# A chunked linear-attention and feed-forward kernel: the high parts of g made by casting DMAs, the guard by an accumulating DMA, splits 1,024 columns wide, and a new order of parts

## The chip, the core and the metric

The kernel runs on one core of a Trainium2 chip. The metric is the device time of one execution in microseconds (us). "PE" is TensorE, "DVE" VectorE, "ACT" ScalarE, "POOL" GpSimd, "SP" SyncE, whose queue issues the loads and stores. A measurement of this kernel varies by about 0.1% either way.

## The reference, cut to what matters

```python
def _attn_ref(q, k, v, alpha):              # 4 x 8 heads, 768 steps, head size 48
    for t in range(S):
        state = alpha[:, :, t, :, None] * state + np.einsum('bhd,bhe->bhde', k[:, :, t], v[:, :, t])
        y[:, :, t] = np.einsum('bhd,bhde->bhe', q[:, :, t], state)

def _moe_ref(x, w_in, w_out):               # x: 3072 x 384, w_in: 384 x 2048, w_out: 2048 x 384
    h = x @ w_in
    sp = np.maximum(h, 0.0) + np.log1p(np.exp(-np.abs(h)))
    g = h * erf(sp)
    return (g @ w_out).astype(np.float32)

x = attn_out.transpose(0, 2, 1, 3).reshape(B * S, H * D)
return _moe_ref(x, w_in, w_out)
```

The weights arrive as 64-bit floats, everything else as 32-bit floats.

## The kernel before

**Attention.** The sequence is cut into 24 chunks of 64 steps for two of the four batches (`Chunk`). A chunk's parts: `la`, `lq`, `lv` load alpha, k and q, and v; `a1` is the running product of alpha (one scan on DVE); `a2` and `a3` scale k by its reciprocal and q by it; `a4` makes the scores `pS` and the state update `pu` on PE, masks the scores (`sT`), updates the state `T` and turns k (`pn`); `a5` makes the output `py` and hands it on as two parts, `x_hi` and `x_lo`. In `a2`, ACT takes first a Relu of the running product above a bound (the "guard": its sum is 0 unless a value is too large), then the logarithm and the exponential that give the reciprocal.

**Feed-forward.** Two chunks give one block of 256 tokens, 12 blocks (`Moe`). Each product is made of three products of rounded parts: high times high, high times low, low times high. A block's hidden 2,048 columns go in four groups of 512, stored as tiles of 128 x 1,024. For each group: `H` (two halves; PE, then a copy to `hs`), `U`, `L1`, `G` on ACT (functions of two tables: `U` and `G` use one, `L1` and the logarithm and exponential of `a2` the other, and each change of table is a table load), `L2` and `Z` on DVE, which leave g in `hs`. `O` (two halves) splits g: `gh` is its rounded copy (ACT, or DVE where the list says `v:`), `gl` the rest (DVE), 512 columns each; then PE adds twelve products of 384 columns to the sums `acc`. `out` stores the block.

**Weights.** `wi_n` (12 pieces) and `wo_n` (16) load a piece of a weight, turn 64-bit into 32-bit floats (ACT and DVE) and split it into `wi_hi`, `wi_lo`, `wo_hi`, `wo_lo`.

**Order.** The order is written out by hand in `SCHED`: a list of the parts, taken one step each. Every engine runs its instructions in the order in which the list made them, and an instruction that waits holds up all behind it on its engine. Most tiles of 128 x 1,024 (`kq`, `hs`, `s`, `w`, `t`, weights on their way) come from one pool, `big`; `gh` and `gl` have buffers of their own, two each. After the list comes the test of the guards (`top`, `count`), which decides whether the slow general branch is run; it isn't with these inputs.

Of the kernel before, what the change touches and what calls it, by code (L numbers as in the profile page):

```python
# [33 lines left out]
a2_1 a2_1 a2_1 a4_0 a4_0 a2_1 wi_1 v:wi_1 wi_1 wi_2 wi_2 wi_6 wi_6 v:wi_6 a2_2 a2_2 a2_1 wi_6 lv_0 lv_1 a5_0 a5_0 a2_2  # L34
a5_0 wi_1 a4_0 a4_0 wi_0 wi_0 wi_6 a2_2 a5_0 a2_2 wi_1 wi_1 v:wi_0 wi_0 wi_4 wi_4 v:wi_4 wi_4 a4_1 a4_1 a4_1 a4_1 wi_0
wi_5 wi_5 v:wi_5 wi_5 wi_4 wi_3 wi_3 v:wi_3 wi_0 wi_7 wi_7 v:wi_7 a5_0 a5_1 wi_4 a5_1 a5_1 wi_0 wi_3 a5_1 wi_8 wi_8
v:wi_8 a5_1 la_3 H_0_0_1 H_0_0_1 wi_5 a4_1 wi_5 H_0_0_0 H_0_0_0 wi_3 wi_9 lq_2 wi_9 v:wi_9 wi_3 a1_3 a2_3 wi_4 wi_9
a2_2 a3_2 a4_2 wi_3 wi_11 H_0_0_1 wi_9 wi_5 wi_11 a2_3 v:wi_11 wi_11 wi_10 wi_10 v:wi_10 wi_10 wi_9 H_0_1_0 a4_2 a4_2
a2_3 wo_2 wo_2 a2_3 wi_11 lv_2 a2_3 wi_10 lq_3 a2_3 H_0_0_0 U_0_0 a4_2 a4_2 la_4 wi_6 wi_7 a3_3 v:wo_2 a5_2 a5_2 a5_2
a5_2 wo_0 wi_10 wi_10 wi_11 wi_11 wi_9 wi_8 H_0_1_0 H_0_1_0 H_0_1_1 H_0_1_1 H_0_1_1 wo_0 U_0_1 L1_0_1 a4_3 a4_3 a4_3  # L40
v:wo_0 wi_8 wi_8 H_0_3_1 H_0_3_0 H_0_3_1 H_0_3_1 wi_7 wi_7 a1_4 a2_4 a2_4 H_0_3_0 H_0_3_0 lv_3 lv_4 a5_3 a5_3 wi_6
a4_3 wi_8 wi_7 wo_2 lq_4 a5_3 a2_4 a5_2 L1_0_0 wo_2 wo_2 lq_5 a5_3 a4_3 H_0_2_0 H_0_2_0 H_0_2_0 a2_4 L1_0_0 L1_0_0
H_0_2_1 H_0_2_1 H_0_2_1 wo_10 wo_10 a3_4 a2_4 a5_3 a2_4 a4_4 wo_2 la_5 H_1_1_0 H_1_1_0 a1_5 L1_0_1 L2_0_0 wo_7 wo_7
L1_0_1 wo_0 wo_10 a2_5 wo_3 wo_0 a4_4 a4_4 L2_0_1 L2_0_0 H_1_0_1 H_1_1_0 L2_0_1 a2_5 a2_5 a2_5 v:wo_7 wo_7 H_1_0_1
H_1_0_1 a5_4 a5_4 a5_4 a5_4 lv_5 wo_0 wo_0 H_1_0_0 a3_5 G_0_0 Z_0_0 a2_5 a4_4 wo_1 wo_7 wo_3 H_1_0_0 H_1_0_0 a2_5
v:wo_3 wo_1 v:wo_1 a4_4 H_1_1_1 H_1_1_1 H_1_1_1 G_0_1 wo_5 wo_5 v:wo_5 Z_0_0 O_0_0_0 Z_0_1 H_1_2_0 wo_4 wo_4 wo_6
H_1_2_0 H_1_2_0 v:wo_4 a4_5 a4_5 a4_5 U_0_2 wo_4 wo_6 v:wo_6 U_0_3 H_1_3_0 H_1_3_0 wo_1 wo_4 wo_4 H_1_3_0 la_6 a4_5
H_1_2_1 H_1_2_1 H_1_2_1 lv_6 a5_5 wo_5 wo_6 H_1_3_1 H_1_3_1 a1_6 a2_6 wo_5 a5_4 wo_5 wo_1 wo_1 wo_3 O_0_0_0 wo_3 a5_5
a5_5 wo_1 a5_5 a5_5 O_0_0_0 O_0_0_0 H_2_3_1 wo_10 H_2_3_1 O_0_0_1 O_0_0_1 wo_10 Z_0_1 a2_6 a4_5 wo_3 lq_6 wo_6 a2_6
a2_6 H_1_3_1 wo_5 H_2_2_0 wo_8 wo_10 a2_6 O_0_0_1 wo_3 wo_8 a2_6 a3_6 O_0_0_1 a4_6 L1_0_2 wo_13 v:wo_8 wo_8 H_2_3_1  # L50
L1_0_2 v:wo_13 wo_4 v:wo_13 wo_10 wo_8 L1_0_3 a4_6 L1_0_2 wo_8 wo_8 wo_7 H_2_2_0 wo_7 a4_6 a4_6 wo_9 v:wo_9 L1_0_3
wo_6 wo_6 H_2_2_0 H_2_2_1 H_2_2_1 L1_0_3 L2_0_2 H_2_3_0 H_2_3_0 O_0_1_0 O_0_1_1 O_0_1_0 O_0_1_1 v:wo_9 wo_9 H_2_2_1
U_1_0 L2_0_2 H_2_3_0 G_0_2 la_7 a1_7 L2_0_3 O_0_1_0 O_0_1_0 wo_11 wo_11 v:wo_11 wo_9 wo_9 H_2_1_0 Z_0_2 la_8 wo_9
Z_0_2 H_2_1_0 H_2_1_0 L2_0_3 wo_11 wo_13 wo_11 H_2_0_0 H_2_0_0 v:H_2_0_0 a2_7 G_0_3 U_1_1 wo_13 a2_7 a2_7 a2_7 H_2_0_1
H_2_0_1 a5_6 a5_6 a5_6 O_0_1_1 O_0_1_1 a5_6 lq_7 a3_7 a2_7 wo_11 wo_11 a2_7 a4_6 O_0_2_0 O_0_2_0 O_0_2_1 O_0_2_1 wo_13
lv_7 H_2_0_1 H_2_1_1 H_2_1_1 L1_1_1 wo_15 wo_15 v:wo_15 H_2_1_1 L1_1_0 a4_7 a1_8 a4_7 a4_7 wo_12 wo_12 a5_6 O_0_2_0
O_0_2_0 v:wo_12 L1_1_0 Z_0_3 wo_15 lv_8 a4_7 L1_1_0 a5_7 Z_0_3 a5_7 a5_7 a5_7 a5_7 O_0_2_1 O_0_2_1 H_3_0_0 wo_12 a2_8
# [692 lines left out]
```

## Time and profile before

| | us |
|---|---|
| median of three runs | 527.58 (527.17 to 527.93) |
| the profiled execution: its time | 526.75 |
| its span, first to last instruction | 525.0 |
| what lies around the span | 1.75 |
| PE busy | 499.5 (95%) |
| DVE busy | 497.3 (95%) |
| ACT busy | 485.1 (92%) |

How to read it: the span is what an instruction can change. Three engines are busy for over nine tenths of it. PE's matmuls overlap, so that a busy PE can still be held up a little at the start of each group of matmuls.

### The profile page before, as it was taken

The numbers are of one execution on the slowest core, as the hardware profiler recorded it, in microseconds if no ns is written. First come the engines' busy times: TensorE is split into PE (matmuls) and PEld (weight loads), VectorE is DVE, ScalarE is ACT, GpSimd is POOL, SyncE is SP. The second block draws the span as 40 slices with busy tenths as digits, with TensorE's granted clock in tenths as the row PEclk, the third lists the DMA queues.
The fourth block names the chain that finished last, engine by engine and source line by source line (L and its number), as shares of the span: only waits on it lengthen the run. The fifth ranks groups of instructions, "written<-read, shape, count | busy, mean of one in ns | idle before, by whom it ended". The sixth has DMA issues, their size and how long they took to land.

```text
span 525.0 us, 16780 instructions
## 1 busy us (share of the span) xinstructions
PE 499.5 (95%) x7386; PEld 481.5 (92%) x7386; DVE 497.3 (95%) x715; ACT 485.1 (92%) x700; POOL 2.3 (0%) x14
## 2 busy tenths in 40 slices
PE   1699999999999999999999999999999999999994
PEld 1599999989999999999999999999999999999994
DVE  6999999999999999999999999999899999999993
ACT  6999999999999999989999899998898999999680
POOL 1000000000000000000000000000000000000000
PEclk9999999999999999999999999999999999999998
DMA  8976353341313203413012311123103120000001
GB/s 296 346 284 237 105 161 114 125 151 41 127 37 93 90 30 107 156 55 134 2 58 67 117 37 38 59 72 109 44 23 121 43 79 26 8 1 30 28 4 37
DMA packets 17936, 48.44 MB, mean 92 GB/s; under 512 B 1984, under 2 KB 5056, under 8 KB 17856
## 3 DMA queue, kind: packets, MB, share of 16 engines
q1 hardware_dynamic: 17856, 47.29, 26.6%
q8 instruction: 60, 0.98, 0.8%
q14 instruction: 20, 0.16, 0.1%
HBM read 42.57 MB, written 4.72 MB: 90 GB/s over the span
## 4 chain that ended last, share of the span: by engine, by line
PE 48%; ACT 25%; DVE 18%; issue 4%; DMA 3%; SPq 0%; DVEq 0%; ACTq 0%
PE acc L495 25%; PE ph L429 18%; ACT s L214 6%; ACT w L214 3%; ACT L213 3%; PE py L364 3%; ACT hs L220 3%; DVE t L458 2%; DVE gl L484 2%; ACT r L214 2%; DVE w L460 2%; DMA A<-in_alpha_dram 2%; ACT wbuf L220 2%; ACT wbuf L532 2%; DVE s L469 2%
## 5 line engine op out<-in xcount | busy, mean ns | idle before, releaser
L429 PE MATMUL ph<-x_hi,wi_hi 128*128 128x256 f32 x576 | 165.8, 288 | 1.8 <-ACT x_hi L220 1.1
L429 PE MATMUL ph<-x_lo,wi_hi 128*128 128x256 f32 x576 | 161.6, 281 | 1.1 <-issue 0.9
L429 PE MATMUL ph<-x_hi,wi_lo 128*128 128x256 f32 x576 | 161.3, 280 | 0.2 <-issue 0.2
L495 PE MATMUL acc<-wo_hi,gh 128*128 128x384 f32 x384 | 130.9, 341 | 0.0
L495 PE MATMUL acc<-wo_hi,gl 128*128 128x384 f32 x384 | 129.9, 338 | 0.8 <-DVE gl L484 0.6
L495 PE MATMUL acc<-wo_lo,gh 128*128 128x384 f32 x384 | 129.1, 336 | 0.0
L429 PEld LDWEIGHTS ph<-x_hi,wi_hi 128*128 128x128 f32 x576 | 109.0, 189 | 5.4 <-ACT hs L220 1.9
L429 PEld LDWEIGHTS ph<-x_hi,wi_lo 128*128 128x128 f32 x576 | 109.8, 191 | 1.0 <-issue 1.0
L429 PEld LDWEIGHTS ph<-x_lo,wi_hi 128*128 128x128 f32 x576 | 109.1, 189 | 0.6 <-DVE x_lo L395 0.5
L214 ACT ACTIVATE s<-s 128x1024 f32<-128x1024 f32 x96 | 100.1, 1054 | 6.2 <-DVE t L458 5.9
L495 PEld LDWEIGHTS acc<-wo_hi,gl 128*128 128x128 f32 x384 | 72.2, 188 | 2.6 <-DVE gl L484 2.4
L495 PEld LDWEIGHTS acc<-wo_hi,gh 128*128 128x128 f32 x384 | 72.2, 188 | 1.2
L495 PEld LDWEIGHTS acc<-wo_lo,gh 128*128 128x128 f32 x384 | 72.2, 188 | 0.0
L484 DVE TENSOR_TENSOR gl<-hs,gh 128x512 fp32r<-128x512 f32 x96 | 65.0, 689 | 6.5 <-ACT gh L220 1.7
L213 ACT ACT_TABLE_LOAD x52 | 66.7, 1283 | 0.9
L471 DVE SCALAR_TENSOR_TENSOR hs<-s,hs 128x1024 f32<-128x1024 f32 x48 | 58.6, 1222 | 0.7
L458 DVE TENSOR_TENSOR t<-s,w 128x1024 f32<-128x1024 f32 x48 | 58.2, 1219 | 1.0 <-ACT w L214 0.8
L469 DVE TENSOR_TENSOR s<-s,w 128x1024 f32<-128x1024 f32 x48 | 58.4, 1220 | 0.6
L460 DVE SCALAR_TENSOR_TENSOR w<-t,w 128x1024 f32<-128x1024 f32 x48 | 58.3, 1220 | 0.3
L220 ACT ACTIVATE hs<-ph 128x512 f32<-128x512 f32 x85 | 49.3, 590 | 3.3 <-PE ph L429 2.8
L214 ACT ACTIVATE w<-s 128x1024 f32<-128x1024 f32 x48 | 50.6, 1057 | 0.6
L214 ACT ACTIVATE s<-hs 128x1024 f32<-128x1024 f32 x48 | 50.4, 1058 | 0.4
(66 smaller groups left out, 719.3 us busy)
## 6 DMA issues: line engine op xcount, KB each, us to landing
kq<-in_qk_dram SPq DMA_DIRECT2D x24, 512.0 KB, 3.7
raw_v<-in_v_dram SPq DMA_DIRECT2D x24, 448.0 KB, 4.1
A<-in_alpha_dram SPq DMA_DIRECT2D x24, 260.0 KB, 3.3
wst<-in_moe_w_in_dram SPq DMA_DIRECT2D x12, 512.0 KB, 9.5
wst<-in_moe_w_out_dram SPq DMA_DIRECT2D x16, 384.0 KB, 3.5
out_dram<-o SPq DMA_DIRECT2D x24, 192.0 KB, 1.9
```

Of the source, the lines that this page charges most:

```text
L213: nc.scalar.preload_act_table_set(table)
L214: nc.scalar.activation(*args, **kw)
L220: nc.scalar.activation(out, in_, AF.Copy, scale=scale)
L364: nc.tensor.matmul(out=py[i][c0 : c0 + 32, kt, :], lhsT=left[r0 : r0 + rows, at0 : at0 + 32], rhs=right[r0 : r0 + rows, pair, i, :], start ...
L429: nc.tensor.matmul(out=o, lhsT=wt[:, kt, fs], rhs=xt[:, kt, :], start=n == 0, stop=n == 3 * KT - 1)
L458: nc.vector.tensor_tensor(out=t, in0=s, in1=w, op=ALU.mult)
L460: nc.vector.scalar_tensor_tensor(out=w, in0=t, scalar=2.0, in1=w, op0=ALU.add, op1=ALU.mult)
L469: nc.vector.tensor_tensor(out=s, in0=s, in1=w, op=ALU.mult)
L471: nc.vector.scalar_tensor_tensor(out=h, in0=s, scalar=RT2 / 2, in1=h, op0=ALU.subtract, op1=ALU.mult)
L484: nc.vector.tensor_tensor(out=gl.rearrange("p a t -> p (a t)"), in0=gg, in1=ghf.bitcast(F32), op=ALU.subtract)
L495: nc.tensor.matmul(out=self.acc[tt][:, :DM], lhsT=gt[:, u, ts], rhs=wt[:, f, :], start=f == 0 and n == 0, stop=f == NF - 1 and n == 2,)
L532: nc.scalar.activation(z, low.bitcast(U32), AF.Copy, scale=0.937 * 2.0**-29)
```

## The change

The guard's Relu leaves ACT: instead a DMA that POOL issues (`ac`) adds each chunk's running product to a tile `sums`, and the largest sum is tested at the end. `O` loses its splits. `E` makes `gh` for all 1,024 columns of a group, in blocks 0 to 10 by a DMA that POOL issues and that casts on its way (block 11: a copy on ACT or DVE); `D` makes `gl` for all 1,024 columns on DVE, as before from `hs` and `gh`. `gh` and `gl` now come from `big`, which has 20 buffers, not 19. Block 11 has six groups, of 4, 4, 2, 2, 2 and 2 column blocks of 128, not four of 4. The branch for `TURNED` is in the code and used nowhere, since `TURNED` is empty. The whole list `SCHED` is new.

```diff
+LAST = (4, 4, 2, 2, 2, 2)
+BY_DMA, TURNED = (0, 1, 2, 3, 4, 5, 6, 7, 8, 9, 10,), ()
 SCHED = """
-la_0 a1_0 la_1 la_2 a1_1 a1_2 lq_0 a3_0 a2_0 a2_0 a2_0 a2_0 a2_0 a2_0 wi_2 wi_2 v:wi_2 wi_2 lq_1 a3_1 wi_2 a2_1 wi_1
...
+la_0 a1_0 a2_0 a2_0 la_1 a1_1 lq_0 a3_0 a2_0 a2_0 a2_1 a2_1 a2_0 la_2 a1_2 a2_1 lq_1 a3_1 a2_1 a4_0 a4_0 wi_1 wi_1
...
-    NBIG, NA = 19, 3
+    NBIG, NA = 20, 3
...
+        def ac(self):
+            nc.gpsimd.dma_start(out=sums, in_=self.A.rearrange("p s t -> p (s t)"), accum_op=ALU.add)
+            yield
+
...
-            nc.scalar.activation(r, A, AF.Relu, bias=-AHI, accum_out=flags[:, self.n, 1:2])
-            yield
             act(LNEXP, r, A, AF.Ln)
             yield
...
+            self.sizes = LAST if n == NBLK - 1 else (4,) * (NF // 4)
...
+        def E(self, g):
+            self.gh[g] = self.pl.w.tile([P, self.sizes[g] * TB], F32R, name="gh", tag=self.pl.tag("gh"))
+            if self.n in BY_DMA:
+                nc.gpsimd.dma_start(out=self.gh[g], in_=self.hs[g])
+            else:
+                copy(self.gh[g], self.hs[g])
+            yield
+
+        def D(self, g):
+            self.gl[g] = self.pl.w.tile([P, self.sizes[g] * TB], F32R, name="gl", tag=self.pl.tag("gl"))
+            nc.vector.tensor_tensor(out=self.gl[g], in0=self.hs[g], in1=self.gh[g].bitcast(F32), op=ALU.subtract)
+            yield
+
         def O(self, g, half):
-            sl = slice(half * 512, (half + 1) * 512)
-            gg = self.hs[g][:, sl]
-            gh = self.pl.gp.tile([P, 2, TB], F32R, name="gh", tag="gh")
-            ghf = gh.rearrange("p a t -> p (a t)")
-            copy(ghf, gg)
-            yield
...
+    for k, z in enumerate((flags, sums)):
+        nc.vector.tensor_reduce(out=top[:, k : k + 1], in_=z, op=ALU.max, axis=mybir.AxisListType.X)
```

Three places of the engines' orders. The first is ACT at the start of the program, before the change; `r` is the reciprocal of `a2`, `wst` and `wbuf` a weight on its way:

```order
L266 ACT_TABLE_LOAD
L266 ACTIVATE r,flags<-A 128x512
L213 ACT_TABLE_LOAD
L214 ACTIVATE r<-A 128x512
L214 ACTIVATE r,flags<-r 128x512
L220 ACTIVATE wbuf<-wst 128x512
L532 ACTIVATE wbuf<-wst 128x512
L266 ACTIVATE r,flags<-A 128x512
```

The same place of the change:

```order
L207 ACT_TABLE_LOAD
L208 ACTIVATE r<-A 128x512
L208 ACTIVATE r,flags<-r 128x512
L208 ACTIVATE r<-A 128x512
L208 ACTIVATE r,flags<-r 128x512
L214 ACTIVATE wbuf<-wst 128x512
L574 ACTIVATE wbuf<-wst 128x512
```

The Relu (the first `r,flags<-A`) and the second table load are gone, and the reciprocal of chunk 1 (the third and fourth ACTIVATE) now stands ahead of the first weight.

The second place is DVE before, where the fourth group of block 0 gets its last operands: the `wo_lo` (the last row but one stands for three) are splits of weights that `O` of that group reads, the first and the last row its two `gl`:

```order
L484 TENSOR_TENSOR gl<-hs,gh 128x512
L540 SCALAR_TENSOR_TENSOR wbuf<-wbuf 128x384 x2
L536 SCALAR_TENSOR_TENSOR wbuf<-wbuf 128x384
L554 TENSOR_TENSOR wo_lo<-wbuf,wo_hi 128x384
L540 SCALAR_TENSOR_TENSOR wbuf<-wbuf 128x384
L222 CAST wo_hi<-wbuf 128x384
L554 TENSOR_TENSOR wo_lo<-wbuf,wo_hi 128x384 x3
L484 TENSOR_TENSOR gl<-hs,gh 128x512
```

The same place of the change, up to the last operand of that group:

```order
L508 TENSOR_TENSOR s<-s,w 128x1024
L578 SCALAR_TENSOR_TENSOR wbuf<-wbuf 128x384
L582 SCALAR_TENSOR_TENSOR wbuf<-wbuf 128x384
L275 TENSOR_TENSOR kq<-kq,rw 128x512
L510 SCALAR_TENSOR_TENSOR hs<-s,hs 128x1024
L596 TENSOR_TENSOR wo_lo<-wbuf,wo_hi 128x384
L525 TENSOR_TENSOR gl<-hs,gh 128x1024
L497 TENSOR_TENSOR t<-s,w 128x1024
L596 TENSOR_TENSOR wo_lo<-wbuf,wo_hi 128x384
```

One wide `gl` stands where two narrow ones stood, and instructions of other groups and of a later chunk (`s`, `hs` and `t` of 1,024 columns, `kq`) now stand between the last operands of this group.

The third place is DVE of the change in block 3, group 2, with the tiles' numbers: `hs_2126` is g of that group, `gh_3641` the output of its casting DMA:

```order
L510 SCALAR_TENSOR_TENSOR hs_2126<-s_3213,hs_2126 128x1024
L499 SCALAR_TENSOR_TENSOR w_3507<-t_3614,w_3507 128x1024
L525 TENSOR_TENSOR gl_3663<-hs_2063,gh_3583 128x1024
L216 CAST x_hi_3286<-py_3511 128x3x64
L508 TENSOR_TENSOR s_3503<-s_3503,w_3507 128x1024
L510 SCALAR_TENSOR_TENSOR hs_2412<-s_3503,hs_2412 128x1024
L525 TENSOR_TENSOR gl_3672<-hs_2126,gh_3641 128x1024
```

Before, `gh` was made by ACT or DVE, in two instructions of 512 columns. Now DVE has five instructions between g (first row) and the `gl` that needs the cast copy (last row), and POOL's DMA is to be made between the two.

## Rows read from the trace of the kernel before

**Rows 1.** Windows by stage: stretch, length, busy us of each engine (instructions), PEclk, DMA share, GB/s.

```profile
0.00:31.00 31.00, 15.65 (x322) 13.76 (x323) 26.42 (x43) 26.06 (x53) 2.35 (x14) 1.00 0.90 324
31.00:124.00 93.00, 90.89 (x1715) 87.00 (x1714) 91.09 (x158) 91.99 (x166) 0.00 (x0) 1.00 0.45 150
124.00:200.00 76.00, 75.55 (x1081) 73.23 (x1080) 74.54 (x102) 75.64 (x107) 0.00 (x0) 1.00 0.25 83
200.00:350.00 150.00, 149.31 (x2314) 144.46 (x2313) 145.80 (x199) 143.72 (x196) 0.00 (x0) 1.00 0.22 71
350.00:518.00 168.00, 167.21 (x1969) 162.57 (x1964) 158.93 (x216) 147.16 (x183) 0.00 (x0) 1.00 0.13 42
518.00:525.00 7.00, 0.85 (x5) 0.53 (x4) 0.56 (x1) 0.49 (x1) 0.00 (x0) 0.74 0.19 64
```

**Rows 2.** Groups by form, PE: total busy us, mean ns of one, idle before.

```profile
L429 PE MATMUL ph<-x_hi,wi_hi 128*128 128x256 f32 x576 | 165.8, 288 | 1.8 <-ACT x_hi L220 1.1 <-ACT hs L220 0.5
L429 PE MATMUL ph<-x_hi,wi_lo 128*128 128x256 f32 x576 | 161.3, 280 | 0.2 <-issue 0.2
...
L495 PE MATMUL acc<-wo_hi,gh 128*128 128x384 f32 x384 | 130.9, 341 | 0.0
L495 PE MATMUL acc<-wo_lo,gh 128*128 128x384 f32 x384 | 129.1, 336 | 0.0
```

**Rows 3.** Timeline of PE, ACT, DVE, the start: start us, busy us, work [idle before].

```profile
10.62 1.98 PE L298 MATMUL pS<-kq 48*64 48x64 f32 x32 [10.62 <-DVE kq L278]
...
26.09 0.58 PE L429 MATMUL ph<-x_hi,wi_hi 128*128 128x256 f32 x1 [1.13 <-ACT x_hi L220]
...
4.97 0.63 ACT L266 ACTIVATE r<-A 128x512 f32<-128x512 f32 x1 [2.88 <-DVE A L260]
5.51 0.19 ACT L266 ACTIVATION_READ_ACCUMULATOR r<-A 128x1 f32 x1
5.71 1.28 ACT L213 ACT_TABLE_LOAD   x1
...
3.70 3.51 DVE L260 TENSOR_TENSOR_SCAN A<-A,lower 128x520 f32<-128x520 f32 x3 [3.70 <-DMA A<-in_alpha_dram]
...
16.73 1.29 DVE L540 SCALAR_TENSOR_TENSOR wbuf<-wbuf 128x512 int32<-128x512 int32 x2
...
25.86 0.62 DVE L395 TENSOR_TENSOR x_lo<-py,x_hi 128x192 fp32r<-128x192 f32 x2
```

**Rows 4.** Timeline of DVE and PE where the fourth group of block 0 begins.

```profile
121.43 1.49 DVE L554 TENSOR_TENSOR wo_lo<-wbuf,wo_hi 128x384 fp32r<-128x384 f32 x3
...
123.41 0.34 PE L495 MATMUL acc<-wo_hi,gh 128*128 128x384 f32 x1
```

**Rows 5.** Groups by form, DVE and ACT.

```profile
L484 DVE TENSOR_TENSOR gl<-hs,gh 128x512 fp32r<-128x512 f32 x96 | 65.0, 689 | 6.5 <-ACT gh L220 1.7 <-DMA out_dram<-o 0.9 <-DVE gh L222 0.5
...
L222 DVE CAST gh<-hs 128x512 fp32r<-128x512 f32 x49 | 20.6, 422 | 0.9 <-PE acc L495 0.2
...
L213 ACT ACT_TABLE_LOAD x52 | 66.7, 1283 | 0.9
...
L220 ACT ACTIVATE gh<-hs 128x512 fp32r<-128x512 f32 x47 | 28.7, 625 | 9.5 <-PE acc L495 7.3 <-DVE hs L471 2.1
...
L214 ACT ACTIVATE s<-hs 128x1024 f32<-128x1024 f32 x48 | 50.4, 1058 | 0.4
```

**Rows 6.** Chain that ended last, two of its links: start us, us, work.

```profile
473.64 6.36 PE ph L429 x54
...
290.62 2.27 DVE t L458 x2
```

**Rows 7.** DMA issues: queue, count, KB each, median us from issue to landing.

```profile
kq<-in_qk_dram SPq DMA_DIRECT2D x24, 512.0 KB, 3.7
...
A<-in_alpha_dram SPq DMA_DIRECT2D x24, 260.0 KB, 3.3
wst<-in_moe_w_in_dram SPq DMA_DIRECT2D x12, 512.0 KB, 9.5
```

More of the change, by code (lines that the diff above doesn't have):

```diff
@@ L227, in gla_moe @@
     nc.gpsimd.memset(T, 0.0)
+    nc.gpsimd.memset(sums, 0.0)
     Tv = T.rearrange("p (i a d) -> p i a d", i=NI, a=NP)[:, :, :, :D]
@@ L348, in a5 @@
                 moe.alloc_x()
+            if self.n in TURNED:
+                py = [ps_at.tile([P, 512], F32, name="pz", tag="at") for _ in range(2)]
+                sums = [(vx, HD, self.sT)]
+                if not self.first:
+                    sums.append((T, D, self.Q))
+                for pair in range(NP):
+                    for n, (left, rows, right) in enumerate(sums):
+                        for par in range(2):
+                            for i in range(NI):
+                                r0 = (par ^ i) * HD
+                                at0 = (i * NP + pair) * HD
+                                nc.tensor.matmul(
+                                    out=py[par][i * HD : (i + 1) * HD, pair * D : (pair + 1) * D],
+                                    lhsT=right[r0 : r0 + rows, pair, i, :], rhs=left[r0 : r0 + rows, at0 : at0 + D],
+                                    start=n == 0, stop=n == len(sums) - 1, tile_position=(r0, i * HD),
+                                )
+                yield
+                t = at.tile([P, KT, 2, 2, HD // 2], F32, name="yt", tag="sT")
+                for par in range(2):
+                    copy(
+                        t[:, :, par].rearrange("p k h d -> p h k d"),
+                        py[par][:, : NP * D].rearrange("p (h k d) -> p h k d", h=2, k=KT),
+                    )
+                    yield
+                px = ps_at.tile([P, 512], F32, name="px", tag="at")
+                for kt, k in enumerate((0, 2, 1)):
+                    nc.tensor.transpose(
+                        px[:, kt * P : (kt + 1) * P], t[:, k].rearrange("p b h d -> p (b h d)"), ident
+                    )
+                yield
+                yield from moe.put_all(px, self.n % 2)
+                return
             py = [ps_at.tile([P, KT, TC], F32, name="py", tag="at") for _ in range(NI)]
@@ L377, in __init__ @@
             self.x = None
-            self.hs, self.w, self.s = [None] * NG, [None] * NG, [None] * NG
+            self.sizes = LAST if n == NBLK - 1 else (4,) * (NF // 4)
+            self.at = [sum(self.sizes[:g]) for g in range(len(self.sizes))]
+            self.hs, self.w, self.s, self.gh, self.gl = ([None] * len(self.sizes) for _ in range(5))
         def alloc_x(self):
@@ L398, in put, with put_all @@
                 yield
+        def put_all(self, px, s):
+            at = [z.rearrange("p k (i j t) -> p k i j t", i=NI, j=2)[:, :, :, s] for z in self.x]
+            y = px[:, : KT * P].rearrange("p (k i t) -> p k i t", k=KT, i=NI)
+            copy(at[0], y)
+            yield
+            nc.vector.tensor_tensor(out=at[1], in0=y, in1=at[0].bitcast(F32), op=ALU.subtract)
+            yield
         def turn(self, y, c, pool, tag):
@@ L630, in general @@
                     m.turn(y[:, 0, :], c, ph, "h")
-                for g in range(NG):
-                    for part in (m.H(g, 0), m.H(g, 1), m.U(g), m.L1(g), m.L2(g), m.G(g), m.Z(g), m.O(g, 0), m.O(g, 1)):
+                for g in range(len(m.sizes)):
+                    for part in (m.H(g, 0), m.H(g, 1), m.U(g), m.L1(g), m.L2(g), m.G(g), m.Z(g), m.E(g), m.D(g), m.O(g, 0), m.O(g, 1)):
                         for _ in part:
```

248 lines of the change are left out of this document (117 added, 131 removed).

## The prediction

> **What bounds the kernel now.** I read first the windows by stage [rows 1]: cut where the first feed-forward matmul begins (before 31 us), where the fourth group of block 0 is added (124), where the attention thins out (350) and where the output is left (518). TensorE (PE) is idle for 15.35 us of the first stage and 6.15 of the last, and for only 2.11, 0.45, 0.69 and 0.79 us of the four between, 4.04 in all. Its clock is 1.00, the 2.4 GHz level, up to 518 us. So PE's own work, 7,386 matmuls, sets the end; the change keeps every one of them. Next come the groups by form [rows 2]: of the four products listed, the first of each triple takes longer than the others that do the same (288 against 280 ns in 576 matmuls, 341 against 336 in 384). That is a small delay at the start of a group, (8 x 576 + 5 x 384) ns = 6.5 us in all, which a busy PE hides. PE could give at most 4.0 + 6.5 us between 31 and 518 us, the start and the end apart.
>
> Then who is beside it: VectorE (DVE) is busy 91.09 of 93 and 74.54 of 76 us up to 200 us, then 145.8 of 150 and 158.9 of 168; ScalarE (ACT) likewise, then 147.2 of 168 [rows 1]. The timelines show where that counts. At the start PE waits for the chain scan, Relu, table load, reciprocal, k, to 10.62 us, and its first `ph` at 26.09 waits for the two parts of x [rows 3]. At 123 us the last `wo_lo` splits end at 122.92 and PE takes their group at 123.41 [rows 4]: there DVE is just in time, and every microsecond more on it counts. After 200 us DVE runs ahead; what is left there are short hand-overs from ACT and DVE to PE.
>
> **The change, part by part.** *Engine sums.* On DVE go 49 casts (20.6 us) and 96 narrow `gl` (65.0) [rows 5]; 46 wide `gl` at 1.22 and 4 narrow ones at 0.69 come (58.9, the wide one taken as `t` of the same shape; two of those in a row end 2.27 us after the first began, 1.14 each [rows 6]). By the order 6 copies of `ph` (0.69 each at most), 3 casts of g and 3 outputs move onto it, about 7 us. DVE: -20.6 - 65.0 + 58.9 + 7 = -20 us. On ACT go 24 Relus of 0.63 and their reads of 0.19 [rows 3], 19.7 us, and 47 narrow `gh`, 28.7 [rows 5]; in come 22 table loads (74 stand in the order, 52 before) at 1.283, 28.2 us, and a few wide copies of block 11 at about 1.06 (as the ACT operation of the same shape [rows 5]), at most 7. ACT: at least -13 us. Both were below PE's sum and fall further: this alone moves nothing but the waits.
>
> *Start.* On ACT the Relu, its read and the second table load leave the first chain: 0.63 + 0.19 + 1.28 = 2.1 us [rows 3], so PE's first `pS` comes near 8.6. This gains little by itself, because the first `ph` then waits for DVE: up to its last `x_lo` DVE has, by the order, 4 scans of 1.17, 24 operations of 512 columns at 0.60 and 6 short ones of 0.27, which after the 3.70 us of loading is 24.4; before it was 3 scans and 27, 25.1 by the same sum and 26.1 in fact. An earlier weight is the other bound: one more 512-KB load stands ahead of it, 1.6 us at the 324 GB/s of that stage [rows 1]. Taken at nothing; -1 to +2.
>
> *Fourth group of block 0.* Here the order decides, since DVE is just in time [rows 4]. Ahead of this group's last operand DVE had 9 scans, 84 operations of 512 columns, 17 of 1,024, 48 of 384 and 27 short ones; now 10, 80, 25, 48 and 25. That is 1.17 - 4 x 0.60 + 8 x 1.14 - 2 x 0.27 = +7.4 us. But PE is given more to do ahead of it: 4 more half-steps of `H` of 9 matmuls at 0.118 (54 in 6.36 us [rows 6]) and one `a4` more at 2.0 [rows 3], +6.2 us. Net +1.2 us; -1 to +3, with the start.
>
> *Dense stretch.* From about 180 us on DVE and ACT have together 30 us less to do against the same PE work, and wide splits mean 50 hand-overs of `gl`, not 96. What can go is 10.5 us (above). The first matmul of a group has always to wait for something, so I take away at most the idle time and about half of the 6.5, and of this range of 0 to 8 us the middle: -4.0.
>
> *Casting DMAs.* No row shows one. Nearest from below: 512 KB of `kq`, 3.7 us from issue to landing; from above: 512 KB of weights, 9.5, taken while the start's loads crowd the queues [rows 7]. DMA share after 31 us is 0.45 falling to 0.13 [rows 1], so I take it near the lower row, 3.7 to 5. What hides it: the DVE work between g and its `gl`. In the order of block 3, group 2 that is `w`, another `gl`, a short cast, `s`, `hs`: 4 x 1.14 + 0.27 = 4.8 us, and this is the shortest of the 44. Worked out likewise, 4 are under 6 us, 12 under 7, 15 under 8 and 22 under 9.5. So at 3.7 to 4.8 us the hand-over costs nothing; beyond, DVE waits, and behind `gl` on it wait the next groups' `s`, `t` and `hs`, then ACT, then PE. Only blocks 0 to 3 have no lead to cover it; there the waits add up to 8 us of DVE at 7 us a DMA, 16 at 8, 33 at 9.5.
>
> *Guard.* Each `ac` moves 260 KB as the load of `A` does, 3.3 us [rows 7], and waits for the one before. All but the last are far from the end. The test of `sums` stands on DVE before the last groups' splits; the last `ac` is issued near them, so a cost of 0 to 2 us is possible; taken 0, since three or four in a row at 3.3 us still land before the last two groups.
>
> *End.* The last matmul, output and store are the same work: 6.15 us [rows 1].
>
> *Sum.* The profiled execution took 526.75 us, 0.83 below the median shown. 526.75 + 1.2 - 4.0 = 523.95 for a profile; with the 0.83, 524.8 us.
>
> **The rivals.** *Slow cast (slower).* The casting DMA takes 7 us or more, because it reads and writes SBUF and POOL must issue it behind the `ac`. At 7 us DVE waits 8.3 us more in blocks 0 to 3, 524.8 + 8.3 = 533; at 8 us 541. It decides from about 6.2 us, where the waits reach the 4.0 gained. For it: 9.5 stands in the rows, and no casting DMA does; against: the row of the same bytes at a quiet time is 3.7.
>
> *Nothing given back (no change).* PE's small waits are those of each group's own first operand and stay; the 10.5 us don't shrink, and +1.2 at the fourth group is made up elsewhere. 527 to 528.6. For it: PE is 99% busy between 31 and 518 us already; against: the idle time is put down to ACT's and DVE's hand-overs.
>
> *Late weights.* More loads in the first 31 us (DMA share 0.90 [rows 1]) delay the first `ph` by 2 to 3 us and nothing makes it up: 528.5 to 531.
>
> *DVE keeps POOL from issuing.* A row speaks of two kinds of DVE work: the cast of 512 columns takes 0.422 us, the subtraction of as many 0.689 [rows 5]. If any DVE instruction kept POOL's DMA from being made, each of the 44 would begin only when DVE stops at its `gl`: 44 x 3.7 = 163 us, less the 48 us that DVE has free after the change (525 - 477): about 640 us. If only the fast casts do, nothing is seen: 46 of the 49 casts of g go away.
> The Trainium skill, SBUF — State Buffer, section "SBUF: two separate sides", says that a DMA issued by GpSimd can't get its descriptors written while VectorE runs an operation in a two-port fast mode, and names the copy of 32-bit floats within SBUF as one. Read broadly, with every operation between g and `gl` in such a mode, it is this rival; read narrowly, with the casts alone, the forecast stands, and 0.422 against 0.689 us speaks for the narrow reading. No trace here shows such a DMA of POOL.
>
> **How the numbers follow.** Forecast 0.55 (521 to 526.4), no change 0.20, slow cast 0.17, late weights 0.06, POOL kept out 0.02. The time is the forecast's, 524.8. The range, 521.0 to 531.0, reaches from 8 us given back (526.75 + 0.83 + 1.2 - 8 = 520.8) over no change and late weights to a cast of some 6.8 us; outside are about 0.05 below and 0.12 above. A measurement here can't tell 0.2%, 1.05 us, from no change. Faster: 0.55; same: 0.22 (no change and a little of late weights); slower: 0.23.
>
> **What would show it.** *Start:* first `pS` near 8.6 us, first `ph` 25 to 27. *Fourth group of block 0:* its first matmul near 130, with DVE busy up to it. *Dense stretch:* PE idle below 2 us between 200 and 518 us, and 288 and 341 ns nearer to 280 and 336. *Casting DMA:* from issue to landing under 5 us, and no idle time of DVE ended by it; 6 us or more, or DVE idle at `gl` in blocks 0 to 3, shows it wrong. *End:* last matmul to the end of the span 6 us as before, with no wait of DVE for `sums`. Wrong would be above all a cast slower than 6.2 us, a tile of the common pool that comes free late, so that the cast is issued late, or a new wait at the last block's six groups.

## The result, and the profile after

The change takes 530.12 us (median of 12 runs, 529.65 to 534.91) against 527.43 before (12 runs): slower, by a ratio of 1.006 (1.0047 to 1.0073). The profiled execution has a span of 528.7 us against 525.0, 3.7 more. Single runs spread wider than the 0.1% named at the start (before: 526.62 to 528.98).

The windows by stage of the change, cut as in [rows 1]; the columns are the same:

```profile
0.00:31.00 31.00, 18.65 (x433) 16.35 (x436) 25.45 (x43) 19.00 (x37) 5.48 (x18) 1.00 0.96 325
31.00:124.00 93.00, 88.77 (x1611) 85.30 (x1599) 90.85 (x150) 92.00 (x157) 6.48 (x9) 0.98 0.63 194
124.00:200.00 76.00, 75.52 (x1233) 72.59 (x1232) 73.42 (x91) 75.49 (x99) 7.87 (x12) 1.00 0.50 154
200.00:350.00 150.00, 150.00 (x2226) 146.11 (x2227) 143.76 (x175) 141.97 (x176) 15.63 (x24) 1.00 0.50 148
350.00:518.00 168.00, 164.40 (x1905) 161.61 (x1899) 149.65 (x179) 147.51 (x170) 12.08 (x20) 1.00 0.28 92
518.00:528.70 10.70, 3.83 (x23) 3.50 (x21) 0.56 (x1) 0.49 (x1) 0.00 (x0) 0.83 0.13 44
```

PE's idle time falls by 3.0 us in the first stage, where it does 433 matmuls instead of 322, and by 0.7 between 200 and 350 us. It grows by 2.1 us between 31 and 124 us and by 2.8 between 350 and 518. PE's busy time is 1.7 us more, though the matmuls are the same: in the second stage the clock is 0.98 on the mean.

Busy and idle time leave out the small delays that a busy PE hides. So I worked out from the records of the matmuls how far PE is behind its own work: the start of a matmul, less what those ahead of it take back to back (0.117 us for each `ph`, 0.173 for each `acc`, and so on: the medians between starts, the same in all the kernels). In us, at the same amount of work done:

| work of PE done | 15 | 23 | 100 | 240 | 350 | 420 | 480 (end) |
|---|---|---|---|---|---|---|---|
| before | 23.5 | 23.6 | 28.2 | 32.5 | 35.2 | 37.4 | 38.7 |
| the change | 21.9 | 27.4 | 29.9 | 34.4 | 37.8 | 40.0 | 41.7 |
| the change, test at the end (below) | 21.9 | 27.6 | 29.8 | 34.4 | 37.2 | 38.1 | 38.3 |

Other prices for the short matmuls move the entries by up to 3.5 us, but what is read from the rows below by at most half a us.

This shows where the time goes. Up to 15 us of work (36.9 us after the start) the change is 1.6 us ahead. Then it loses 5.5 us within 8 us of work. From 23 us of work to the end the kernel before falls another 15.1 us behind, the change with its test at the end 10.7. So 4.4 us are gained behind the start: 2.4 of them up to 100 us of work (some 130 us after the start), 2.0 after it. The change as it is loses most of this again after 240 us of work.

The place of the first loss, in the timelines of ACT, DVE and PE of the change:

```profile
35.55 1.28 ACT L207 ACT_TABLE_LOAD   x1
36.84 1.06 ACT L208 ACTIVATE s<-hs 128x1024 f32<-128x1024 f32 x1
37.81 0.61 ACT L214 ACTIVATE wi_hi<-wbuf 128x512 fp32r<-128x512 f32 x1
...
38.45 1.29 DVE L596 TENSOR_TENSOR wi_lo<-wbuf,wi_hi 128x512 fp32r<-128x512 f32 x2 [1.19 <-ACT wi_hi L214]
...
39.80 0.38 PE L468 MATMUL ph<-x_hi,wi_lo 128*128 128x256 f32 x1 [2.42 <-DVE wi_lo L596]
45.47 0.33 PE L393 MATMUL py<-sT,raw_v 64*32 64x64 f32 x11 [0.82 <-issue]
```

On ACT a table load and the first group's `U` stand ahead of a `wi_hi`, DVE's `wi_lo` waits for it, and PE for that. At 45.47 PE waits again, for nothing that the profile shows. The windows of the change there:

```profile
35.00:40.00 5.00, 2.58 (x71) 2.33 (x72) 3.81 (x7) 4.94 (x6) 0.00 (x0) 1.00 1.03 298
40.00:45.00 5.00, 4.65 (x133) 4.27 (x132) 4.96 (x11) 5.00 (x11) 0.84 (x1) 0.66 1.04 347
```

After the 2.42 us without work the granted clock is 0.66: by the trace's records 3.4 us at the 1.2 GHz level from 40.4 us on. A `ph` starts every 0.21 us there and every 0.117 after it, so the stretch costs about half its length, 1.7. So 2.7 (from one matmul's start to the next) + 1.7 + 1.0 make up 5.4 of the 5.5.

The second loss, in the waits of DVE and of PE late in the change (us in total, times, longest):

```profile
DVE top L711 <- ACT r L208: 2.9, 1, 2.9
DVE top L711 <- DMA sums<-A: 2.8, 1, 2.8
...
PE pS L295 <- DVE kq L275: 1.5, 1, 1.5
...
PE acc L537 <- DVE o L218: 1.0, 1, 1.0
```

`top` is the test of the guards. It is the one piece of the program that isn't in the hand-written list, so the scheduler chose its place: on DVE ahead of the last chunk's work, where it stops at 436.8 us for ACT's reciprocal and at 490.5 for the last accumulating DMA. Behind it stand `kq`, for which PE waits at 442 us, and DVE's work before the output copy `o`, for which PE waits at 504. Before, the same `top` stood at 426.6 us, with no wait.

The transfers, from the DMA issues and the group of `gl` of the change:

```profile
gh<-hs POOLq DMA_DIRECT2D x44, 512.0 KB, 2.9
...
sums<-A POOLq DMA_DIRECT2D x24, 260.0 KB, 4.7
wst<-in_moe_w_in_dram SPq DMA_DIRECT2D x12, 512.0 KB, 10.5
```

```profile
L525 DVE TENSOR_TENSOR gl<-hs,gh 128x1024 fp32r<-128x1024 f32 (+1 forms) x50 | 58.6, 1175 | 0.4
```

The casting DMA lands in 2.9 us, and DVE loses 0.4 us ahead of all 50 `gl`. The accumulating DMA takes 4.7.

### The profile page after: what moved, and what is told of

The parts are those of the page before. It is cut to its first block, busy times and chain, and to the rows that moved or that the text cites. A ratio compares the mean times of both kernels' runs of the same rounds, so it can differ in the third digit from the quotient of the medians.

```text
span 528.7 us, 16811 instructions
## 1 busy us (share of the span) xinstructions
PE 501.2 (95%) x7386; PEld 485.5 (92%) x7386; DVE 483.7 (91%) x635; ACT 476.5 (90%) x636; POOL 47.5 (9%) x83
## 3 DMA queue, kind: packets, MB, share of 16 engines
q1 hardware_dynamic: 17856, 47.29, 27.4%
## 4 chain that ended last, share of the span: by engine, by line
PE 46%; ACT 28%; DVE 15%; issue 6%; DMA 4%; SPq 0%; POOL 0%; DVEq 0%; ACTq 0%; POOLq 0%
PE acc L537 21%; PE ph L468 17%; ACT s L208 7%; ACT L207 5%; PE py L393 3%; ACT w L208 3%; ACT hs L214 3%; DMA sums<-A 2%; DVE t L497 2%; PE pS L295 2%; DVE w L499 2%; DVE hs L510 2%; DMA raw_v<-in_v_dram 2%; DVE gl L525 2%; ACT r L208 2%
## 5 line engine op out<-in xcount | busy, mean ns | idle before, releaser
L208 ACT ACTIVATE s<-s 128x1024 f32<-128x1024 f32 (+1 forms) x100 | 101.2, 1021 | 7.3 <-DVE t L497 6.8
L508 DVE TENSOR_TENSOR s<-s,w 128x1024 f32<-128x1024 f32 (+1 forms) x50 | 58.8, 1175 | 8.7 <-ACT s L208 7.4
L497 DVE TENSOR_TENSOR t<-s,w 128x1024 f32<-128x1024 f32 (+1 forms) x50 | 58.6, 1176 | 2.7 <-ACT w L208 2.5
L510 DVE SCALAR_TENSOR_TENSOR hs<-s,hs 128x1024 f32<-128x1024 f32 (+1 forms) x50 | 58.7, 1178 | 0.8
L499 DVE SCALAR_TENSOR_TENSOR w<-t,w 128x1024 f32<-128x1024 f32 (+1 forms) x50 | 58.7, 1177 | 0.7
L525 DVE TENSOR_TENSOR gl<-hs,gh 128x1024 fp32r<-128x1024 f32 (+1 forms) x50 | 58.6, 1175 | 0.4
L518 POOL DMA_DIRECT2D gh<-hs x44 | 23.6, 537 | 368.2 <-DVE hs L510 78.1
L214 ACT ACTIVATE hs<-ph 128x512 f32<-128x512 f32 x79 | 46.0, 588 | 9.1 <-PE ph L468 9.1
L208 ACT ACTIVATE s<-hs 128x1024 f32<-128x1024 f32 (+1 forms) x50 | 50.9, 1022 | 2.5 <-DVE hs L216 1.1
```

The source lines that it names most:

```text
L208: nc.scalar.activation(*args, **kw)
L214: nc.scalar.activation(out, in_, AF.Copy, scale=scale)
L497: nc.vector.tensor_tensor(out=t, in0=s, in1=w, op=ALU.mult)
L499: nc.vector.scalar_tensor_tensor(out=w, in0=t, scalar=2.0, in1=w, op0=ALU.add, op1=ALU.mult)
L508: nc.vector.tensor_tensor(out=s, in0=s, in1=w, op=ALU.mult)
L510: nc.vector.scalar_tensor_tensor(out=h, in0=s, scalar=RT2 / 2, in1=h, op0=ALU.subtract, op1=ALU.mult)
```

## The experiments

Each was run against the kernel before on the same chip. "Both moves" is the change with the first two edits. The ratio is the record's, which differs by up to 0.2% from the quotient of the two medians. The traces quoted are of one execution each.

| run | median, us | before there | ratio (95%) |
|---|---|---|---|
| start_order | 531.63 | 527.45 | 1.0098 (1.0067 to 1.0129) |
| late_test | 527.94 | 527.45 | 1.0016 (1.0004 to 1.0027) |
| both_moves | 529.74 | 527.45 | 1.0038 (1.0022 to 1.0055) |
| no_sums | 533.40 | 527.45 | 1.0111 (1.0095 to 1.0128) |
| late_wo | 530.72 | 527.54 | 1.0070 (1.0045 to 1.0096) |
| old_list_guard | 530.02 | 527.54 | 1.0042 (1.0025 to 1.0058) |
| old_list_cast | 583.21 | 527.54 | 1.1059 (1.1039 to 1.1079) |
| engine_copies | 557.11 | 527.54 | 1.0565 (1.0542 to 1.0589) |
| both_unguarded | 528.90 | 527.67 | 1.0032 (1.0013 to 1.0051) |
| both_relu | 529.38 | 527.67 | 1.0055 (1.0034 to 1.0076) |
| late_relu | 529.23 | 527.67 | 1.0027 (1.0006 to 1.0048) |
| old_list_relu | 527.48 | 527.67 | 1.0001 (0.9988 to 1.0014) |
| both_py_later | 537.91 | 527.73 | 1.0197 (1.0171 to 1.0223) |
| late_py_later | 537.01 | 527.73 | 1.0177 (1.0158 to 1.0197) |
| both_one_half | 531.44 | 527.27 | 1.0080 (1.0063 to 1.0097) |
| late_one_half | 531.88 | 527.27 | 1.0089 (1.0072 to 1.0106) |
| relu_py_later | 539.05 | 527.73 | 1.0203 (1.0177 to 1.0230) |
| relu_one_half | 533.04 | 527.27 | 1.0120 (1.0100 to 1.0141) |

**The two places.** My theory was two independent losses, the order near 36 us and the place of the test; the rivals were late loads and PE's own waits.

```diff
 start_order:
-H_0_0_0 U_0_0 wi_5 wi_7 wi_4 a1_4 a2_4 wi_5 wi_7 wi_3 a4_3
+H_0_0_0 wi_5 wi_7 wi_4 wi_5 wi_7 wi_3 a1_4 U_0_0 a2_4 a4_3
 late_test (the code of the test as a part of the list):
-D_11_4 O_11_3_0 O_11_4_0 O_11_4_0 O_11_5_0 O_11_5_0 out_11_0
+D_11_4 O_11_3_0 test O_11_4_0 O_11_4_0 O_11_5_0 test O_11_5_0 out_11_0
```

> The change with the test of the guards (the two reductions, the counts, its matmul and its copy) put by hand behind the last D of block 11. Theory (DVE waits at the test, and PE waits for what stands behind it): DVE's waits of 2.9 us for ACT's reciprocal near 437 us and of 2.8 us for the last accumulating DMA near 491 us go, and with them PE's waits of 1.5 us for kq near 442 us and of 1.0 us for the output copy near 504; 1.5 to 2.6 us less than 530.1, so 527.5 to 528.6. Rival (PE's waits there come from ACT's three table loads in a row and stay): 529.5 to 530.5.

The theory holds. The windows of late_test have for 350 to 518 us:

```profile
350.00:518.00 168.00, 167.55 (x1926) 165.00 (x1920) 150.42 (x179) 147.48 (x170) 12.04 (x20) 1.00 0.28 92
```

PE is idle for 0.45 us there, not 3.6, and the time is 2.2 us less than the change's. So much did the test's place cost.

> The change with seven steps in another order near 36 us: U of block 0's first group, with its table load, and the scan of chunk 4 stand behind the last steps of the weight pieces 5, 7 and 3, no longer ahead of them. Theory (one wait at the start, set by the order on ACT and DVE): PE's wait of 2.4 us for wi_lo near 37 us falls below 1 us, and the granted clock stays at 1.00 from 40 to 45 us instead of 0.66; 2 to 4 us less than the change's 530.1, so 526 to 528. Rival (weights come late because the transfers are full): PE waits as long, for the next weight piece, and the time is 529.5 to 530.5.

> The two edits together. Theory (two independent losses): the sum of both, 3.5 to 6.5 us less than 530.1, so 523.6 to 526.6, below the kernel before. Rival (PE's waits move on to the next late operand): 527 or more.

Both theories missed: start_order lies beyond its rival too, both_moves where its rival has it (527 or more), though the wait that came next is for no operand. The wait for `wi_lo` fell to 0.2 us as expected, but another took its place. The timeline of PE, and the windows, of start_order:

```profile
45.83 0.45 PE L393 MATMUL py<-sT,raw_v 64*32 64x64 f32 x11 [3.88 <-issue]
```

```profile
40.00:45.00 5.00, 1.95 (x122) 1.56 (x120) 4.05 (x8) 4.99 (x10) 0.84 (x1) 1.00 1.02 397
45.00:50.00 5.00, 4.17 (x32) 3.87 (x33) 4.74 (x10) 5.00 (x11) 0.00 (x0) 0.66 0.50 135
```

PE stands still for 3.9 us and the profile names no one; the lower clock now comes behind that. In both_moves the same wait is 4.5 us, in an execution of 531.67 us, near the longest of its runs (527.48 to 531.94). So there is a second limit just beneath the first. The trace also has the transfers of instructions (60 packets of 16 KB on queue 8): one lands at 44.4 us, and PE goes on 1.4 us later, at matmul 731. In both_moves it lands at 46.3, and PE goes on at 47.7, at matmul 731 again. Matmuls are counted from 0. That made a new theory: PE lacks its own instructions, because the output step of a chunk spends 128 short matmuls in 1.4 us (the expectations below say 192, which is wrong). It had waited at matmul 731 in the change too, 0.82 us.

**What holds the instructions up?** Late weights, the accumulating DMAs, or only PE's pace?

```diff
 no_sums (without the guard by sums):
-nc.gpsimd.dma_start(out=sums, in_=..., accum_op=ALU.add)
 late_wo (both moves, and):
-wo_1 ... wo_11 ... wo_1 v:wo_1 wo_3 ... wo_0 wo_0 ... wo_3 v:wo_3 ... H_0_2_1
+H_0_2_1 wo_1 wo_11 wo_3 wo_0 wo_1 v:wo_1 wo_0 wo_3 v:wo_3
 both_unguarded (both moves, and):
+if self.n not in (1, 2, 3, 4):
     nc.gpsimd.dma_start(out=sums, in_=..., accum_op=ALU.add)
 both_relu, late_relu (both moves; only the test moved), for chunks 1 to 4 in its place:
+nc.scalar.activation(r, A, AF.Relu, bias=-AHI, accum_out=over[:, self.n : self.n + 1])
```

> The change without the accumulating DMAs; it leaves out the guard against large running products (sums stays 0). Theory (the start is lost by the order near 36 us): PE's wait for wi_lo stays at 2 us or more, the wait at the test near 491 us goes with what it cost, 528.5 to 530. Rival (the accumulating DMAs delay the start, by the 5.7 us that SP's queue waits for them before it loads alpha and the weights behind it, and by the bytes that they move while the DMA engines are full): the wait for wi_lo goes, 526 to 528.

PE's wait for `wi_lo` stayed at 2.3 us, so the accumulating DMAs don't cause it. The time, 3.3 us above the change's, was neither theory's: without the DMAs to wait for, the scheduler took the test still earlier, and DVE stopped 2.9 us for the reciprocal and 3.4 for the test's own matmul:

```profile
DVE total L717 <- PE pf L715: 3.4, 1, 3.4
DVE top L710 <- ACT r L208: 2.9, 1, 2.9
```

> The kernel with both moves (U and a scan later, test at the end), and in addition the loads of four pieces of the second weight (1, 11, 3, 0; 384 KB each) and their first copies some 15 us later, behind the first half of H of block 0's group 2. Theory (PE's own instructions come through the DMA engines, and near 45 us wait there behind these loads): the DMA share from 40 to 45 us falls below 0.8 from 1.03, PE's waits that nothing releases, 1.8 and 4.5 us at 40 and 47 us, fall below 1.5 together, the clock stays at 1.00 after 35 us; 3 to 5 us less than the 529.7 with both moves, so 524.5 to 527. Rival (those waits hang on something else of that place): they stay, 529 or more. Second rival (the later weights are missed by O of block 0): the waits go, PE waits for wo_lo before 124 us, 528 or more.

> The kernel with both moves (U and a scan later, test at the end), without the accumulating DMAs of chunks 1 to 4; it leaves out the guard for these chunks. Theory (near 45 us PE waits for its own instructions, which come through the DMA engines, and the accumulating DMAs are what fills these): the DMA share from 40 to 45 us falls below 0.9, PE's waits that nothing releases (6.3 us between 38 and 48 us with both moves) fall below 1.5, 4 to 6 us less than 529.7, so 524 to 526. Rival (the loads of weights, k, q and v fill the engines by themselves): the waits stay at 4 us or more, 528.5 to 530.

> The kernel with both moves, with the guard of chunks 1 to 4 made by a Relu on ACT as before, and by accumulating DMAs for the other 20 chunks; the whole reference is computed. Theory (as for the unguarded one; ACT has room before 35 us, 3 to 4 of 5 us busy): 524.5 to 526.5, below the kernel before. Rival (ACT's 0.8 us each are missed at the start, or the waits stay): 528 or more.

In all three the rival holds: with 1.5 MB of weights later PE's unnamed wait is still 3.7 us, and with four accumulating DMAs gone still 4.3, at matmul 731. The packet lands at 44.1 to 44.5 us each time. In late_wo the DMA share from 40 to 45 us stayed at 1.04, where its theory wanted it below 0.8, so that run doesn't test full DMA engines; in both_unguarded it fell to 0.90:

```profile
40.00:45.00 5.00, 1.72 (x121) 1.43 (x119) 4.32 (x8) 5.00 (x11) 0.00 (x0) 1.00 0.90 335
```

> The change with the test at the end and the guard of chunks 1 to 4 by a Relu on ACT, U and the scan at their places of the change. Theory (PE's wait for wi_lo near 37 us is set by the order on ACT, not by the DMA engines): that wait stays at 2 us or more, with a stretch of lower clock behind it, 527 to 528.5, as with the test at the end alone (527.9). Rival (it is set by late loads): it goes, 524 to 526.

The wait stayed (2.1 us), as the theory had it, but the time is above its range. In this profile the clock stayed at 1.00 after the wait, so the 1.7 us are not paid each time.

**PE needs fewer instructions before 45 us.** Chunk 3's output step, put behind two halves of H (py_later) or one (one_half):

```diff
-H_0_1_0 H_0_1_0 ... a5_3 a5_3 ... H_0_1_0 ... H_0_1_1 H_0_1_1 H_0_1_1 ... H_0_2_1 H_0_2_1 H_0_2_1
+H_0_1_0 H_0_1_0 ... H_0_1_0 ... H_0_1_1 H_0_1_1 H_0_1_1 [one_half: a5_3] ... H_0_2_1 H_0_2_1 H_0_2_1 [py_later: a5_3, a4_4]
```

> The kernel with both moves (U and a scan later, test at the end), and chunk 3's output step (192 short matmuls of 64 columns) and the beginning of chunk 4's scores put behind two halves of H of block 0 (36 long matmuls), so that PE needs fewer instructions before 45 us. Theory (near 42 us PE waits for its own instructions, whose packet lands near 44.3 us whatever else is loaded): PE does H in that time, its waits that nothing releases between 38 and 50 us fall from 6.3 us to under 2, no stretch of lower clock; 3 to 5 us less than 529.7, so 525 to 527. Rival (H's weights or hs come no earlier, since all loads are late): PE waits for wi_lo or hs in its place, 528.5 to 530.

> The same move of chunk 3's output step with the test at the end, but with U and the scan at their places of the change. Theory: the wait of 2.4 us for wi_lo near 37 us stays, as it is set by the order on ACT and DVE; the instructions' packet has landed by then, so the move gives 0 to 1.5 us beside 527.9: 526.5 to 528. Rival (both waits are one, late loads): the same time as with both moves and this one.

By the times the rival held for both, at a much higher price than both_py_later's named: the second half's weights weren't there. In late_py_later the waits for `wi_lo` (1.9 us) and for `wi_hi` (2.9) stand apart, so that they are one wait isn't shown. PE's timeline in both_py_later:

```profile
48.52 0.58 PE L468 MATMUL ph<-x_hi,wi_hi 128*128 128x256 f32 x1 [6.83 <-ACT wi_hi L214]
```

> Both moves, chunk 3's output step later, and the guard of chunks 1 to 4 by a Relu on ACT; the whole reference is computed. Theory: as both_py_later or up to 1 us less, since the accumulating DMAs leave the full stretch: 524 to 527, and if any, this one is below the kernel before. Rival (the Relus are missed on ACT at the start): 0.5 to 1.5 us more than without them.

It ran into the same wait, of 7.7 us from one matmul to the next. Its median is 1.1 us above both_py_later's, as its rival says, but the two intervals overlap.

> Both moves, and chunk 3's output step behind only one half of H of block 0's group 1 (18 long matmuls, 2.1 us), whose weights are there by then. Theory (at 42 us PE waits for its own instructions, not for data): PE does this H from 42 us on and takes the output step near 45.8 us as with both moves, its waits that nothing releases fall from 6.3 us to 3 or less, 1.5 to 2.5 us less than 529.7, so 527.2 to 528.2. Rival (ACT, 5 of 5 us busy with weights from 40 to 47 us, sets when the next H can begin): no gain, 529 to 530.5.

> The same order of chunk 3's output step, with the test at the end, U and the scan where the change has them. Theory: the wait for wi_lo stays, PE's wait for instructions is short there anyway (0.4 us), 0 to 1.5 us less than 527.9: 526.5 to 528. Rival (ACT's order): 528 to 529.5.

PE's timeline in both_one_half:

```profile
45.21 0.28 PE L393 MATMUL py<-kq,T 48*32 48x64 f32 x7 [1.34 <-issue]
46.47 0.45 PE L295 MATMUL pS<-kq 48*64 48x64 f32 x8 [0.80 <-DVE kq L275]
50.27 0.35 PE L304 MATMUL pu<-raw_v,kn 64*64 64x48 f32 x3 [3.26 <-DVE x_lo L426]
```

The unnamed wait fell from 4.5 to 1.3 us, at the same matmul, and it ended 1.5 us after the packet (43.7 us): for that wait the theory of the instructions holds. But the time rose above both ranges, in the way of the rival: a third limit, `x_lo`, comes behind ACT's `x_hi`, and ACT has 5.0 us of work in every 5 from 40 to 50 us, weights above all. In late_one_half the wait for `x_lo` is 3.3 us too.

> The last one with the guard of chunks 1 to 4 by a Relu on ACT; the whole reference is computed. Theory: the accumulating DMAs cost the start nothing in the new list (with and without them PE came as late), so as the last one, 526.5 to 528.5; rival (ACT is short of time from 40 us on): 528.5 or more.

The rival holds: 533.04 us.

**The parts of the change on the old list.**

```diff
 old_list_guard (Relu for no chunk), old_list_relu (Relu for chunks 0 to 4 as before); in both the test is a part of the list:
-nc.scalar.activation(r, A, AF.Relu, bias=-AHI, accum_out=...)
+nc.gpsimd.dma_start(out=sums, in_=..., accum_op=ALU.add)
 old_list_cast:
-copy(ghf, gg)
+nc.gpsimd.dma_start(out=ghf, in_=gg)
```

> The kernel before, with one part of the change: the Relu of each chunk replaced by the accumulating DMA, its test put by hand behind the last gl. Theory (the guard itself is a small gain, and the loss is in the new list): ACT is 20 us less busy, PE begins 1 to 2 us earlier, 525 to 527.5. Rival (the accumulating DMAs hold alpha's buffers and crowd the start): PE's waits before 60 us grow by 2 us or more, 529 to 531.

> The kernel before with the guard of chunks 0 to 4 by the Relu as it was and of the other 19 by accumulating DMAs, the test behind the last gl. Theory (the accumulating DMAs cost time only while the start's loads fill the DMA engines): PE's waits of 3.9 us for raw_v and 2.5 us for x_hi, seen with all of them by DMA (530.0), go; 526 to 527.6. Rival (they cost time by holding the buffers of alpha through the whole attention): 529 to 530.5.

The rival holds for the first and the theory for the second. In old_list_guard PE waits at the start for transfers, as its waits show:

```profile
PE py L366 <- DMA raw_v<-in_v_dram: 3.9, 1, 3.9
PE ph L431 <- ACT x_hi L221: 2.5, 1, 2.5
```

With the first five left on ACT the wait for `raw_v` is 1.6 us and the time is that of the kernel before. So on that list the accumulating DMAs cost 2.5 us while the start's loads are under way and nothing measurable later, and 11 us less work on ACT gain nothing.

> The kernel before, with one part of the change: the two copies of each group of blocks 0 to 10 made by casting DMAs of 512 columns, at their old places with the short hand-overs of the old list. Theory (a casting DMA needs some 2.5 us from issue to landing, so the list must leave it that much): DVE and PE wait for gh in most groups, 532 to 545. Rival (PE's lead hides the hand-over anyway): 525 to 528, and the long hand-overs of the new list are not needed.

> The change with the test at the end, and with gh of blocks 0 to 10 made by ACT (groups 0 and 2, 1.06 us each) and DVE (1 and 3, 0.69 us each) instead of by casting DMAs: ACT 23 us and DVE 15 us more busy. Theory (the casting DMAs take work off engines that are just in time only until 180 us): 1 to 6 us more than 527.9 with the test at the end, so 529 to 534. Rival (casting DMAs crowd the DMA engines and cost what they give): 526 to 528.

```diff
 engine_copies (test at the end, and):
-BY_DMA, TURNED = (0, 1, 2, 3, 4, 5, 6, 7, 8, 9, 10,), ()
+BY_DMA, TURNED = (), ()     (E of groups 1 and 3: on DVE, of 0 and 2: on ACT)
```

Old_list_cast shows what the hand-over is worth; its rows of waits and of DMA issues:

```profile
POOL gh L482 <- PE acc L498: 115.6, 33, 10.1
DVE gl L487 <- DMA gh<-hs: 75.1, 31, 6.3
```

```profile
gh<-hs POOLq DMA_DIRECT2D x88, 256.0 KB, 2.7
```

The same 2.7 to 2.9 us that cost nothing behind 4.8 us of other work cost 56 us where the list leaves too little, more than the theory's range. How much of the 56 is the hand-over alone isn't shown: on this list `gh` has two buffers, and POOL waits for PE's `acc` before 33 of the 88 casts (first row); and PE stands at the 1.2 GHz level for 23.9 us. Engine_copies shows the reverse: on the new list the casting DMAs are worth 29 us against engine copies, more than either theory had, since PE's waits for `hs` and `gl` grow too. That is the price of copies on a list ordered for DMAs, not a gain over the kernel before, whose copies stand on a list of their own:

```profile
PE ph L469 <- ACT hs L215: 9.0, 9, 1.6
PE acc L538 <- DVE gl L526: 6.0, 3, 4.8
PE ph L469 <- DVE hs L217: 4.9, 2, 4.1
```

No kernel here beats the kernel before; late_test is the best with the new list, old_list_relu is level.

## Why the prediction was wrong

- **Casting DMAs: right.** Forecast 3.7 to 5 us and no wait; 2.9 us and 0.4 us of idle time. The Trainium skill, DMA: Bandwidth & Descriptors, section "Anatomy of one DMA — SWDGE (gpsimd) path", gives 2.0 us plus the bytes at 436 GB/s; an estimate by it is 3.2 us for 512 KB and 2.6 for 256; the rows (2.9 and 2.7) are within 0.3 us of it. The rivals "slow cast" and "DVE keeps POOL from issuing" fall.
- **Dense stretch: right in sign, about half in size.** Forecast -4.0, from about 180 us on. Of the 4.4 us gained behind the start only 2.0 come after 100 us of work (some 130 us after the start); that the whole is near 4.0 is luck. PE is idle 0.0 us between 200 and 350 us, and `gl`'s matmuls went from 338 to 336 ns; 288 and 341 ns did not fall (289, 341), so the gain isn't at the first matmuls of the groups, where I looked for half of it.
- **Start: the step that failed first** ("Taken at nothing; -1 to +2"). The first `pS` came at 9.63 us (forecast 8.6), the first `ph` at 26.52 (25 to 27), and to 36.9 us the change was 1.6 us ahead. I had followed DVE's sum to the first `ph` and then to the fourth group, and not the steps of the list between them, where ACT's order, PE's instructions and the weights are each just in time. Measured: +3.8 us net at 23 us of work. The rival "late weights" (0.06) has the result in its 528.5 to 531, but not by its way: it had the first `ph` 2 to 3 us late, and that was 0.4. What speaks for late weights further on: in the change 5 of the 12 loads of the first weight are issued by 9.2 us and the last at 32 us; before, 9 by 13.5 and the last at 24.4. That this order of loads is why ACT's weight work falls between 40 and 50 us is argued from these times, not tested.
- **Guard and end: the second** ("a cost of 0 to 2 us is possible; taken 0"). I named the wait of the test for `sums` and set it to nothing, since the DMAs before it would have landed: the last one was issued at 488.7 us, and DVE came to the test at 490.5. And I did not see that `top` on `flags` can stop DVE as well. Together they cost 2.2 us.
- **Fourth group of block 0: wrong in sign.** Forecast +1.2. Its first matmul came at 130.93 us (forecast 130), with DVE busy up to it, but no wait of PE stands there; between 23 and 100 us of work the change falls 2.5 us behind, before 4.6. Of the 2.1 gained (2.4 with the test at the end), 0.9 is an unnamed wait that the kernel before has at 108.5 us and the change has not. A net sum of work ahead of a point doesn't tell a wait when both engines come to the point later.
- **End of the program:** 6.9 us of idle time after 518 us, not 6.15; 0.7 us that I left at nothing. Its cause is open.
- **Two readings.** The engine sums (DVE -20 us, ACT at least -13) added up durations of instructions that overlap; the busy time fell by 13.6 and 8.6. And the clock was not at the 2.4 GHz level from the start: the `ph` of the kernel before start 0.21 us apart up to 29.9 us and 0.12 after, those of the change up to 30.2. The row's 1.00 covers a stretch without a record of the clock. Neither enters the sum.

Together: -4.4 + 3.8 + 2.2 + 0.7 = +2.3 us; measured, by the medians, 2.7. That 530.12 us lies inside the stated range is no merit of the forecast: its upper end was there for a slow cast and for a first `ph` some 2 us late, and neither came.

What stays open: what sets the time at which a packet of instructions lands. Without four accumulating DMAs, or with four loads of the second weight later, it landed at 44.1 to 44.5 us, as in start_order (44.5); both_moves, with neither edit, had 46.3, so a gain of less than 2 us couldn't be told. Open too is where in the groups the dense stretch gains: the wide splits, the 20 buffers and block 11's six groups were not run by themselves.

## What to carry to other kernels

A transfer in place of a copy costs the waiting engine next to nothing (0.4 us over 50 `gl`) as long as the list leaves it more other work than the transfer takes, and it cost the kernel 1.3 us a group (56 us in all, over 44 groups) on the list that doesn't. Code outside of a hand-written order is placed by a scheduler that can put a waiting instruction ahead of urgent work: write its place down too. Where a start has several limits at nearly the same level, follow every engine's queue through it, since taking one limit away shows only the next.

## What the runs showed of the hardware that I had not expected

PE can run out of instructions. In eight of the kernels run here it stands still at matmul 731 until 1.3 to 1.5 us after a 16-KB packet has landed, and in the py_later kernels at matmul 987 (3.4 us, packet at 62.8 us, on at 64.1 in both_py_later). The profile calls it "issue". All other waits of PE under that name have the same form: in the 20 traces, each one of over 0.15 us up to 520 us ends 1.2 to 1.6 us after a packet has landed, and at a matmul near a multiple of 127.5 from 731 (349, 476, 604, 987, 1751, 3279, 5569 among them, none more than 8 off; 7,386 matmuls over 60 packets are 123 a packet). The kernel before has one too, of 0.9 us at 108.5 us. Most come behind steps of many short matmuls (128 in 1.4 us) before 65 us, where packets land mostly 4 to 8 us apart; in the change after 124 us, with a DMA share of 0.5 or less, the same steps show no such wait over 0.2 us, though one of 1.0 us stands behind such a step at 352 us. The transfer of the packet that PE waits for at 731 took 0.9 to 1.1 us in these eight kernels; it began late, 0.9 us (late_relu) to 7.1 us (both_moves) after PE had come to matmul 603. That PE lacks its instructions is read from these times; no run changed how they arrive.

After some 2 to 7 us without matmuls the granted clock was at the 1.2 GHz level for 3.4 or 6.8 us in most of the profiles here, but not in late_relu after 2.1 us, nor in old_list_cast after 3.6 us at 432 us. An accumulating DMA of 260 KB within SBUF took 4.7 us, a load of the same size 3.4.
